# A fused attention-and-FFN kernel: more softmax tiles on VectorE, with the last integer shift of most batches done by an accumulating DMA

## The chip, the cores and the metric

One core of one Trainium2 chip. The metric is the device time of one execution in microseconds. A kernel was run four or more times beside runs of the kernel before on the same chip; medians are quoted. A ratio compares the mean times of two kernels' runs, matched by rounds, so it is not quite the ratio of the two medians that stand beside it. The profile shows one execution. Its span is some 2 us shorter than the time of the same run. In its views PE is TensorE, PEld are TensorE's weight loads, DVE is VectorE, ACT ScalarE, POOL GpSimd and SP SyncE; a number such as L904 is a line of the kernel. The granted clock is the share of TensorE's full clock that it was given.

## The reference

```python
x = A_x                                  # 1 x 2048 x 512, bf16
xn = _layernorm(x, axis=-1)
return x + _A_ref(xn, A_wq, A_wk, A_wv, A_wo) + _B_ref(xn, B_w1, B_b1, B_w2, B_b2)
# _A_ref: 32 query heads of 16, one shared key and value head;
#   p = softmax(q k^T * 16**-0.5);  o = p v;  o @ wo
# _B_ref: gelu(xn @ w1 + b1) @ w2 + b2, 1792 hidden columns
```

## The kernel before

The scores are made transposed, in tiles of 128 keys by 512 queries: 2048 tiles, in 683 units of three. A unit's three tiles lie in three banks of PSUM, the memory that PE writes to. ScalarE exponentiates them in one instruction, unless one of them is a "D tile". Then ScalarE takes only two, and VectorE makes the third: it rounds the scaled score to an integer whose bits are a coarse exponential in bf16, makes copies of it shifted by four constants, and PE multiplies each copy by a V that is scaled for it. The five products together approximate the exponential. `DTAB` says which units have a D tile (439 of them).

```python
SPL_K = (-51, -26, 0, 26, 51)            # the integer shifts; 0 is the PSUM pass itself

def p1(t, bk):                           # PSUM pass of one D tile
    ...
    dve(lambda e: e.tensor_scalar(Dt[:, KZ, s, :], bank(bk), float(127 * 128) + SPL_D, SPL_MIN, ALU.add, ALU.max), ...)

def close_batch():                       # up to three D tiles make a batch
    n = len(batch)
    s0 = batch[0][1]
    order = [KZ] + [k for k in range(len(SPL_K)) if k != KZ]
    for k in order:
        if k != KZ:
            dve(lambda e, k=k: e.tensor_scalar(Dt[:, k, s0:s0 + n, :], Dt[:, KZ, s0:s0 + n, :], float(SPL_K[k]),
                                               None, ALU.add), ...)
        for t, s in batch:               # PE: one product per copy and tile
            gg, kt, j = tile_of(t)
            pv_mm(gg, j, 1 + k, kt, Dt[:, k, s, :].bitcast(bf), [("D", s, k)])
```

Instructions are not issued in the order in which they are written: a list scheduler simulates all engines with estimates (`occ`, how long an instruction holds its engine, and `lat`, how long after that its result may be used) and writes out a fixed order for each engine. On the chip, an engine runs its instructions in that order, and semaphores make it wait where an estimate was too short. All of a group's products go into one PSUM accumulator.

Of the kernel before, what the change touches and what calls it, by code (L numbers as in the profile page):

```python
# [10 lines left out]
P = 128  # L11
# [27 lines left out]
NE_ND_KB = (25, 8, 3)  # L39
LA = 34  # L40
LB = 105
LY = 9
LP = 121
LS = 107
# [6 lines left out]
DTAB = "...00.20.0022.00.2...202202.22..0.200220..220..0.02.222002.20...2200220.2.0.2220.0...200000..002002.2.00..200220..00.200.0000....02.220.22.0220.02...2.22200022.0.2..220..20200220.20.20.220....22.200.2222.020020...2220.222.0222.0.020......2.2..0..020202....0220.20..0022.02.0...22..2220.2020.22.20...0.020020002...0020...02.00..0002202.022....222.2222.2222.0000..222.0.0222.022.200....00000.2020.00.02.2...22202.2.22.0000.000...2.2200.22..22.20.0...2.2.2.002..020020....220.2200.002.22.000....000020.2200.22200...02202.2.2002..2022...222220..0.2222.0020..22.00002.02.222020....20222...0202..0..2...220....2000.2.0.22....2.2.2.00..2.002020...0.00.2202.02000.00...20022.02.00.202000...."  # L51
# [7 lines left out]
YS = 9  # L59
HA = 40  # L60
HB = 165
# [365 lines left out]
def bass_parallel_sum__grouped_kv_mqa__dense_activation_gelu__prompt_kernel(  # L427
# [27 lines left out]
    NPR = 5  # L455
    NV = 1 + len(SPL_K)
    KZ = SPL_K.index(0)
    GAM = 128.0 / LN2 * 0.25
# [3 lines left out]
    with ExitStack() as es:  # L462
# [4 lines left out]
        ub = sb([P, FT, TBW], bf, "ub")  # L467
        xn = ub[:, 0:8, :]
        xnT = sb([P, DT, S], bf, "xnT")
        wvk = sb([P, DT, 2 * Dh], bf, "wvk")  # L470
        wkp = sb([P, DT, 4, 32], bf, "wkp")
        wq_sb = sb([P, DT, D], bf, "wq_sb")
        wqp = sb([P, DT, HG, 32], bf, "wqp")
# [31 lines left out]
        scr = sb([P, D], bf, "scr")  # L505
# [4 lines left out]
        ksq = sb([P, NT, Dh], f32, "ksq")  # L510
# [5 lines left out]
        Vf = sb([P, NT, Dh], f32, "Vf")  # L516
# [6 lines left out]
        Dt = sb([P, len(SPL_K), ND, TBW], i16, "Dt")  # L523
# [7 lines left out]
        oTp = sb([P, NPR, TBW], bf, "oTp")  # L531
# [41 lines left out]
        def dma(eng, o, i, stream, r=(), w=(), lat=2.2, allow=1.0, **kw):  # L573
            return add(eng, lambda e: e.dma_start(o, i), r, w, dma=stream, occ=0.7, lat=lat, allow=allow, **kw)
# [29 lines left out]
        dve(lambda e: e.memset(wkp[:], 0.0), w=["wkp"], n=256, due=0.0)  # L604
        dve(lambda e: e.memset(wqp[:], 0.0), w=["wqp"], n=512, due=0.1)
# [14 lines left out]
        for v, c in enumerate((1.0,) + SPL_C):  # L620
            setup(lambda e, v=v, c=c: e.memset(V1[:, v, :, Dh:Dh + 1], c), r=["V1"], w=["V1"], due=11.0)
        setup(lambda e: e.memset(sel8[:], 0.0), w=["sel8"], occ=0.3, due=12.0)
# [16 lines left out]
        def ln_batch(ts, how):  # L639
# [4 lines left out]
            if how == "a":  # L644
                for ti in ts:
                    act(lambda e, ti=ti: e.activation(scr[:], x_sb[:, ti, :], ACT.Identity, accum_out=sm[:, ti:ti + 1]),
                        r=[("x", ti)], w=["scr", ("sm", ti)], n=TBW + 250, due=land(ti))
                setup(lambda e: e.tensor_scalar(mean[:, sl], sm[:, sl], 1.0 / D, None, ALU.mult),
                      r=[("sm", ti) for ti in ts], w=mk, occ=0.2)
                setup(lambda e: e.tensor_scalar(nm[:, sl], sm[:, sl], -1.0 / D, None, ALU.mult),  # L650
                      r=[("sm", ti) for ti in ts], w=[("nm", ti) for ti in ts], occ=0.2)
                for ti in ts:
                    act(lambda e, ti=ti: e.activation(scr[:], x_sb[:, ti, :], ACT.Square, bias=nm[:, ti:ti + 1],
                                                      accum_out=sm[:, ti:ti + 1]),
                        r=[("x", ti), ("nm", ti)], w=["scr", ("sm", ti)], n=TBW + 250, due=land(ti))
                setup(lambda e: e.tensor_scalar(ve_b[:, sl], sm[:, sl], 1.0 / D, 1e-5, ALU.mult, ALU.add),
                      r=[("sm", ti) for ti in ts], w=[("ve", b)], occ=0.2)
            else:
                for ti in ts:
                    dve(lambda e, ti=ti: e.bn_stats(stats[:, ti, :], x_sb[:, ti, :]), r=[("x", ti)], w=[("st", ti)],  # L660
                        n=530, due=land(ti) + 1.0)
# [32 lines left out]
        def normed(ti):  # L694
            b, mean_ap = batch_of[ti]
            if XN_ENG[ti] == "d":
                dve(lambda e: e.tensor_scalar(xn[:, ti % 8, :], x_sb[:, ti, :], mean_ap, rstd[:, ti:ti + 1], ALU.subtract, ALU.mult),  # L697
                    r=[("x", ti), ("rstd", b), ("mv", b, ti)], w=[("u", ti % 8)], n=270, due=land(ti) + 2.0)
            else:
                act(lambda e: e.activation(xn[:, ti % 8, :], x_sb[:, ti, :], ACT.Identity, bias=nmr[:, ti:ti + 1],  # L700
                                           scale=rstd[:, ti:ti + 1]),
                    r=[("x", ti), ("rstd", b), ("nmr", b)], w=[("u", ti % 8)], n=TBW + 60, due=land(ti) + 2.0)

        def x_T(ts, bk, eng):
# [5 lines left out]
            for k, ti in enumerate(ts):  # L710
                for d in range(DT):
                    o = (d * n + k) * P
                    add("pe", lambda e, ti=ti, d=d, o=o: e.transpose(pT[:, o:o + P], xn[:, ti % 8, d * P:(d + 1) * P], ident[:]),  # L713
                        r=[("u", ti % 8), "ident"], w=[B(bk)], occ=0.085, due=land(ti) + 3.0)
# [95 lines left out]
        for v, c in enumerate(SPL_C):  # L810
            setup(lambda e, v=v, c=c: e.tensor_scalar(V1[:, 1 + v, :, 0:Dh], Vf[:], c, None, ALU.mult),
# [69 lines left out]
        def p1(t, bk):  # L881
            if not batch and dptr[0] + KB > ND:
# [4 lines left out]
            dve(lambda e: e.tensor_scalar(Dt[:, KZ, s, :], bank(bk), float(127 * 128) + SPL_D, SPL_MIN, ALU.add, ALU.max),  # L887
                w=[B(bk), ("D", s, KZ)], allow=P1_ALLOW, kind="p1")
# [7 lines left out]
        def close_batch():  # L896
            n = len(batch)
            s0 = batch[0][1]
            order = [KZ] + [k for k in range(len(SPL_K)) if k != KZ]
            for k in order:  # L900
                if k != KZ:
                    dve(lambda e, k=k: e.tensor_scalar(Dt[:, k, s0:s0 + n, :], Dt[:, KZ, s0:s0 + n, :], float(SPL_K[k]),  # L902
                                                       None, ALU.add),
                        r=[("D", s0 + i, KZ) for i in range(n)], w=[("D", s0 + i, k) for i in range(n)],  # L904
                        n=n * TBW, mode=4, allow=1.0, kind="post")
                for t, s in batch:
                    gg, kt, j = tile_of(t)
                    pv_mm(gg, j, 1 + k, kt, Dt[:, k, s, :].bitcast(bf), [("D", s, k)])
            del batch[:]

        onorm = {}

        def o_evac(gg):
# [20 lines left out]
            if h or end:  # L934
# [3 lines left out]
                                                r=keys, w=[("oTp", sl)], allow=3.0)  # L938
# [54 lines left out]

        def h_mm(tb, ft, ev=EV_ALLOW):
# [6 lines left out]
        def h_chain(tb, fts, al=3.0):  # L1001
# [3 lines left out]
            uu = ub[:, f0:f0 + n, :]  # L1005
            hk = [("h", s0 + i) for i in range(n)]
            uk = [("u", f) for f in fts]
# [8 lines left out]
        def y_mm(tb, i, start=True, stop=False, bk=7, fts=range(FT), al=1.5):  # L1016
            for ft in fts:
                mm4(bank(bk), ub[:, ft, i * P:(i + 1) * P], w2_sb[:, ft, :], start and ft == fts[0], stop and ft == fts[-1],
                   r=[("u", ft), "w2"], w=[B(bk)], allow=al)

        def wo_mm(tb, i, ps, start=False, bk=7, al=1.5):
            for n, p in enumerate(ps):
                pp = tb * NGR // 2 + p
                hs = [h for h in range(2) if 2 * pp + h < NTB * NGR - 1]
                assert all(2 * pp + h in onorm for h in hs)
# [6 lines left out]
        def store(tb, i):  # L1032
            ti = tb * 4 + i
            dma("sp", of[ti * P:(ti + 1) * P, :], x_sb[:, ti, :], f"d_o{i}", r=[("x", ti)], w=[("ob", i)])

        def out_tile(tb, i):
# [3 lines left out]
            ti = tb * 4 + i  # L1040
            dve(lambda e: e.tensor_tensor(x_sb[:, ti, :], pM, x_sb[:, ti, :], ALU.add), w=[("x", ti)] + M4, allow=EV_ALLOW)
            store(tb, i)

        xpy = x_sb[:, 0:8, :].rearrange("p t d -> p (t d)").bitcast(f32).rearrange("p (t d) -> p t d", d=D)

        def y_tile(tb, i):
            ti = tb * 4 + i
            y_mm(tb, i, al=YT_ALLOW[i])
            wo_mm(tb, i, range(FIN_G), al=YT_ALLOW[i])
            b2_mm(stop=i < 3, al=YT_ALLOW[i])  # L1050
            if i < 3:
                dve(lambda e: e.tensor_tensor(xpy[:, i, :], pM, x_sb[:, ti, :], ALU.add), r=[("x", ti)],
                    w=M4 + [("x", 2 * i), ("x", 2 * i + 1)], allow=EV_ALLOW)
            else:
                mm4(pM, ident, x_sb[:, ti, :], False, False, r=["ident", ("x", ti)], w=[B(7)], allow=YT_ALLOW[i])
# [22 lines left out]
        for tb in range(NTB):  # L1078
            u0 = tb * UPT
            if tb > 0:  # L1080
                for i in range(4):
                    at(u0 + 3 + (YS if tb < NTB - 1 else 9) * i, lambda tb=tb, i=i: out_tile(tb - 1, i), 0.6)
                q_at(tb, 3, u0 + Q3, (2, 3), (4, 5, 6, 7))
            a, b = (HA, HB) if tb < NTB - 1 else (LA, LB)
            if tb == 0:
                a = 18
            nf = FT if tb < NTB - 1 else FT - FIN_F
            for f0 in range(0, nf, 3):
                fts = list(range(f0, min(nf, f0 + 3)))
                for ft in fts:  # L1090
                    at(u0 + a + (b - a) * ft / FT, lambda tb=tb, ft=ft: h_mm(tb, ft), 0.6)
                at(u0 + a + (b - a) * fts[-1] / FT, lambda tb=tb, fts=fts: h_chain(tb, fts), len(fts) * 1.067 + 0.33)
# [3 lines left out]
            else:  # L1096
                for i in range(4):
                    at(u0 + LS + LY * i, lambda tb=tb, i=i: y_tile(tb, i), 0.6)
                fts = list(range(nf, FT))
                for ft in fts:  # L1100
                    at(u0 + LP + ft - nf, lambda tb=tb, ft=ft: h_mm(tb, ft), 0.6)
                if fts:
                    at(u0 + LP + len(fts), lambda tb=tb, fts=fts: h_chain(tb, fts, LAL), (len(fts) * 1.067 + 0.33) * LCO)
# [66 lines left out]
        for i in (0, 1, 3, 2):  # L1170
            ti = tb * 4 + i
            w = [(B(FB[i]), j) for j in range(4)] + ([B(FB[i])] if i < 3 else []) + [("x", ti)]
            if i < 3:
                dve(lambda e, i=i, ti=ti: e.tensor_tensor(x_sb[:, ti, :], bank(FB[i]), xpy[:, i, :], ALU.add),
                    r=[("x", 2 * i), ("x", 2 * i + 1)], w=w)
            else:
                act(lambda e, i=i, ti=ti: e.activation(x_sb[:, ti, :], bank(FB[i]), ACT.Copy), w=w)
            store(tb, i)
# [44 lines left out]
```

## Time and profile before

| | before |
|---|---|
| time, median of 4 runs | 797.58 us (796.94 to 798.07) |
| D tiles; batches | 439; 152 |
| exps of 1536 / of 1024 elements | 243 / 440 |
| shift instructions on VectorE | 608 |
| ScalarE idle in the span | 795.8 - 774.0 = 21.8 us |
| mean granted clock | 0.989 |

ScalarE sets the pace: it is full from 40 to 780 us, its 21.8 idle us lie in the prologue and the tail. The lines that carry this are in the prediction.

### The profile page before, as it was taken

The page shows a single profiled execution, that of the slowest core. Times are in us where ns is not written, and L with a number is a line of the kernel's source. Part 1 is how long each engine was busy: PE and PEld are TensorE (multiplying, and loading weights), DVE is VectorE, ACT ScalarE, POOL GpSimd, SP SyncE. Part 2 cuts the span into 40 slices and gives each one's busy share as a digit, 9 for nine tenths or more (in the row PEclk, how much of TensorE's full clock was granted, in tenths as well). Part 3 has the DMA queues.
Part 4 walks back from the last instruction along what each step waited for, and adds up shares of the span by engine and source line. Part 5 has one row for each costly group of instructions (what it writes and reads, how often), then busy time and mean ns, then how long its engine had stood idle before and what let it go on. Part 6 is the DMA issues. An engine that isn't in the chain of part 4 may idle for free.

```text
span 795.8 us, 20778 instructions
## 1 busy us (share of the span) xinstructions
PE 767.0 (96%) x8759; PEld 240.5 (30%) x8759; DVE 739.8 (93%) x1401; ACT 774.0 (97%) x734; POOL 20.8 (3%) x84
## 2 busy tenths in 40 slices
PE   6799999999999999999999999999999999999998
PEld 4323322232222323322232233322233233323222
DVE  8589999999998959999999889999999998999896
ACT  4899999999999999999999999999999999999995
POOL 6300000000000000000000000000000000000000
PEclk7899999999999999999999999999999999999999
DMA  9101100000000010001000001100001010000001
GB/s 312 41 9 30 23 15 16 17 21 13 12 22 23 23 29 16 17 15 22 17 13 24 20 19 23 22 16 16 19 12 22 24 22 23 16 9 16 16 9 35
DMA packets 30007, 21.17 MB, mean 27 GB/s; under 512 B 16353, under 2 KB 25434, under 8 KB 29914
## 3 DMA queue, kind: packets, MB, share of 16 engines
q1 hardware_dynamic: 28330, 19.28, 9.4%
q8 instruction: 69, 1.13, 0.6%
q10 hardware_dynamic: 1584, 0.56, 0.3%
q14 instruction: 24, 0.20, 0.1%
HBM read 10.98 MB, written 2.35 MB: 17 GB/s over the span
## 4 chain that ended last, share of the span: by engine, by line
ACT 92%; PE 5%; DVE 3%; DMA 0%; issue 0%; DVEq 0%
ACT E L870 88%; ACT ub L1012 3%; PE pAll L891 2%; PE pAll L851 1%; DVE stats L660 1%; PE pAll L567 1%; PE pAll L561 1%; DVE Dt L887 0%; DVE Dt L902 0%; DMA x_sb<-in_A_x_dram 0%; ACT xnT L718 0%; PE pAll L713 0%; ACT KT L732 0%; ACT ub L700 0%; DVE ub L697 0%
## 5 line engine op out<-in xcount | busy, mean ns | idle before, releaser
L870 ACT ACTIVATE E<-pAll 128x1024 bf16<-128x1024 f32 (+1 forms) x683 | 736.7, 1335 | 1.5 <-PE pAll L851 1.3
L891 PE MATMUL pAll<-Dt,V 128*32 128x512 bf16 x2195 | 390.0, 383 | 0.3
L887 DVE TENSOR_SCALAR Dt<-pAll 128x512 int16<-128x512 f32 x439 | 292.9, 680 | 28.9 <-PE pAll L851 28.3
L891 PE MATMUL pAll<-E,V 128*32 128x512 bf16 x1609 | 303.2, 387 | 1.4 <-DVE Of L915 1.2
L902 DVE TENSOR_SCALAR Dt<-Dt 128x1536 int16<-128x1536 int16 (+1 forms) x608 | 297.6, 533 | 0.9
L851 PE MATMUL pAll<-QT,KT 32*128 32x512 bf16 x2048 | 268.3, 386 | 15.0 <-ACT E L870 8.4
L851 PEld LDWEIGHTS pAll<-QT,KT 32*128 32x128 bf16 x2048 | 68.8, 91 | 290.4 <-ACT E L870 222.9
L891 PEld LDWEIGHTS pAll<-Dt,V 128*32 128x32 bf16 x2195 | 105.6, 94 | 107.0 <-issue 54.8
L567 PE MATMUL pAll<-xnT,w_sb 128*32 128x512 bf16 x896 | 128.1, 382 | 0.1
L567 PE MATMUL pAll<-w_sb,ub 128*32 128x512 bf16 x896 | 125.4, 382 | 0.0
L891 PEld LDWEIGHTS pAll<-E,V 128*32 128x32 bf16 x1609 | 70.7, 93 | 77.0 <-issue 59.1
L567 PE MATMUL pAll<-wop,oTp 128*32 128x512 bf16 x256 | 50.8, 381 | 0.0
L998 DVE TENSOR_SCALAR hb<-pAll,b1T 128x512 bf16<-128x512 f32 x56 | 41.5, 740 | 0.8 <-PE pAll L891 0.5
L567 PEld LDWEIGHTS pAll<-xnT,w_sb 128*32 128x32 bf16 x896 | 33.6, 95 | 24.1 <-issue 10.0
L567 PEld LDWEIGHTS pAll<-w_sb,ub 128*32 128x32 bf16 x896 | 32.1, 95 | 11.8 <-issue 5.2
L1184 PE MATMUL pAll<-xnT,zeros 128*32 128x512 bf16 x308 | 33.1, 383 | 0.0
L1012 ACT ACTIVATE ub<-ub 128x1536 bf16<-128x1536 bf16 (+1 forms) x20 | 32.1, 1606 | 0.0
L915 DVE COPY Of<-pAll 128x512 f32<-128x512 f32 x31 | 21.1, 680 | 5.0 <-PE pAll L567 4.1
L567 PE MATMUL pAll<-xnT,wq_sb 128*32 128x512 bf16 x256 | 20.5, 398 | 0.0
L1011 DVE TENSOR_TENSOR ub<-ub,hb 128x1536 bf16<-128x1536 bf16 (+1 forms) x20 | 17.9, 893 | 0.1
L1014 DVE TENSOR_TENSOR ub<-ub,hb 128x1536 bf16<-128x1536 bf16 (+1 forms) x20 | 17.9, 894 | 0.1
L1009 DVE TENSOR_TENSOR ub<-hb 128x1536 bf16<-128x1536 bf16 (+1 forms) x20 | 17.8, 892 | 0.1
(124 smaller groups left out, 242.7 us busy)
## 6 DMA issues: line engine op xcount, KB each, us to landing
OfP<-Of SPq DMA_DIRECT2D x124, 32.0 KB, 1.9
rbP<-rden_rows SPq DMA_DIRECT2D x124, 32.0 KB, 1.8
w_sb<-in_B_w_dram SPq DMA_DIRECT2D x2, 1792.0 KB, 13.5
x_sb<-in_A_x_dram SPq DMA_DIRECT2D x8, 256.0 KB, 6.1
out_dram<-x_sb SPq DMA_DIRECT2D x16, 128.0 KB, 1.7
QT<-qp SPq DMA_DIRECT2D x124, 16.0 KB, 1.8
wq_sb<-in_A_wq_dram ACTq DMA_DIRECT2D x1, 512.0 KB, 6.5
wop<-in_A_wo_dram SPq DMA_DIRECT2D x1, 512.0 KB, 16.3
```

The costliest lines, as they stand in the source:

```text
L567: add("pe", lambda e, c=c, j=j: e.matmul(o[c, :], l[:, c], rh, start=start, stop=stop, tile_position=(0, 32 * j)), r, [(k, j) for k in w] ...
L851: ins = e.matmul(o, l, rh, start=True, stop=True, tile_position=(q0, 0))
L870: exps.append(act(lambda e: e.activation(E[:, s0:s0 + na, :], bank(b0, na).rearrange("p (a n) -> p a n", a=na), ACT.Exp, scale=LN2 / 128.0 ...
L887: dve(lambda e: e.tensor_scalar(Dt[:, KZ, s, :], bank(bk), float(127 * 128) + SPL_D, SPL_MIN, ALU.add, ALU.max), w=[B(bk), ("D", s, KZ)], ...
L891: add("pe", lambda e, a, b: e.matmul(pO[32 * j:32 * j + 32, :], V1[:, v, kt, :], rhs, start=a, stop=b, tile_position=(0, 32 * j)), r=r + [ ...
L902: dve(lambda e, k=k: e.tensor_scalar(Dt[:, k, s0:s0 + n, :], Dt[:, KZ, s0:s0 + n, :], float(SPL_K[k]), None, ALU.add), r=[("D", s0 + i, KZ ...
L915: dve(lambda e: e.tensor_copy(Of[:, i, :], pO), w=["O", ("Of", i)], allow=0.0)
L998: dve(lambda e: e.tensor_scalar(hb[:, ft % 6, :], pM, b1T[:, ft:ft + 1], None, ALU.add), r=["b1T"], w=M4 + [("h", ft % 6)], allow=ev)
L1011: dve(lambda e: e.tensor_tensor(uu, uu, hh, ALU.mult), r=uk + hk, w=uk, n=c, mode=2, allow=al)
L1012: act(lambda e: e.activation(uu, uu, ACT.Tanh, scale=GELU_K), r=uk, w=uk, n=c, allow=al - 0.5, kind="tanh")
L1014: dve(lambda e: e.tensor_tensor(uu, uu, hh, ALU.mult), r=uk + hk, w=uk, n=c, mode=2, allow=al)
L1184: pr.filler = lambda e, j, o: e.matmul((pO if o else pM)[32 * j:32 * j + 32, :], zeros[:, 0:32], xnT[:, 0, 0:TBW], start=not o, stop=not o ...
```

## The change

The intent is to move more exponentials from ScalarE to VectorE, and to pay for it by taking work off VectorE: in most batches the fourth shift is done by a DMA that adds a constant row to the first copy, in place, once the first copy's products have been read. The rest makes room for that: four copies in place of five, twelve slots in place of eight, two FFN activation buffers (the second over x, whose rows are loaded again when they are needed), so that the FFN's work can be spread.

```diff
-DTAB = "...00.20.0022.00.2...          (cut; 439 D tiles)
+DTAB = "....2.002002222.00...          (cut; 473 D tiles)
-NE_ND_KB = (25, 8, 3)
+NE_ND_KB = (22,12,3)
+HP = ((18,160),(180,320),(330,470),(480,590))      # where the FFN's parts go
+YP = (...)
+DM_T = 40                        # the DMA serves batches that end at tile 40 or earlier of a group's 64
+DM_LAT = 4.0
+DM_OCC = 1.0
 ...
-        def dma(eng, o, i, stream, r=(), w=(), lat=2.2, allow=1.0, **kw):
+        def dma(eng, o, i, stream, r=(), w=(), lat=2.2, allow=1.0, accum=False, **kw):
+            if accum:
+                return add(eng, lambda e: e.dma_start(o, i, accum_op=ALU.add), r, w, dma=stream, occ=DM_OCC, lat=lat, allow=allow, **kw)
 ...
+            setup(lambda e: e.memset(kst[:], SPL_K[KORD[-1]]), w=["kst"], occ=0.4, due=12.0)
 ...
+            by_dma = batch[-1][0] % TPG <= DM_T
+            for step, k in enumerate(KORD):
+                b = min(step, len(KORD) - 2)
+                if 0 < step < len(KORD) - 1:
+                    dve(... Dt[:, b, s0:s0 + n, :] = Dt[:, 0, ...] + SPL_K[k] ...)          # shortened
+                elif step:
+                    b = 0
+                    if by_dma:
+                        dma("pool", Dt[:, 0, s0:s0 + n, :], kst[:].unsqueeze(1).to_broadcast([P, n, TBW]), f"d_sh{s0}", r=["kst"], w=[(q, 0) for q in keys],
+                            lat=DM_LAT, accum=True)
+                    else:
+                        dve(lambda e, k=k: e.tensor_scalar(Dt[:, 0, s0:s0 + n, :], Dt[:, 0, s0:s0 + n, :], float(SPL_K[k]), None, ALU.add), ...)
                 for t, s in batch:
                     gg, kt, j = tile_of(t)
-                    pv_mm(gg, j, 1 + k, kt, Dt[:, k, s, :].bitcast(bf), [("D", s, k)])
+                    pv_mm(gg, j, 1 + k, kt, Dt[:, b, s, :].bitcast(bf), [(("D", s), b)])
 ...                              # (cut: second buffer, reload of x, aliased scratch)
```

`DM_OCC` and `DM_LAT` are what the scheduler takes the DMA to need: 1.0 + 4.0 = 5.0 us from its start on GpSimd until PE may read the result. 107 of 169 batches use it, all of three tiles (384 KB).

## The prediction

> **What bounds the kernel now.** I read the page's busy shares first, then the windows (busy time of each engine in stretches of the run), then the chain that ended last, the costliest groups, the waits, and a stretch of VectorE's timeline. The busy shares alone name three suspects:
>
> ```profile
> PE 767.0 (96%) x8759; PEld 240.5 (30%) x8759; DVE 739.8 (93%) x1401; ACT 774.0 (97%) x734; POOL 20.8 (3%) x84
> ```
>
> The windows (columns: stretch, length, then busy us and instruction count of PE, PEld, DVE, ACT, POOL, then clock, DMA share, GB/s) separate them:
>
> ```profile
> 40.00:100.00 60.00, 58.66 (x635) 18.05 (x634) 57.44 (x113) 59.95 (x57) 0.00 (x0) 1.00 0.09 21
> ...
> 200.00:300.00 100.00, 98.64 (x1204) 29.46 (x1203) 87.95 (x169) 100.00 (x94) 0.00 (x0) 1.00 0.09 21
> 300.00:400.00 100.00, 98.49 (x1055) 30.13 (x1054) 98.86 (x185) 100.00 (x94) 0.00 (x0) 1.00 0.08 17
> 400.00:500.00 100.00, 99.47 (x1211) 30.29 (x1211) 92.21 (x179) 100.00 (x95) 0.00 (x0) 1.00 0.08 20
> 500.00:600.00 100.00, 97.39 (x1056) 29.48 (x1054) 99.01 (x180) 99.40 (x93) 0.00 (x0) 1.00 0.07 17
> ...
> 764.00:780.00 16.00, 15.39 (x188) 4.36 (x188) 15.30 (x29) 16.00 (x17) 0.00 (x0) 1.00 0.06 14
> ```
>
> ScalarE is full from 40 to 780 us. VectorE swings between 88% and 99%: idle while the FFN's second matmul runs, full while the FFN's activation chain runs. GpSimd does nothing. The chain of waits agrees, and the groups say what the ScalarE work is:
>
> ```profile
> ACT E L870 88%; ACT ub L1012 3%; PE pAll L891 2%; PE pAll L851 1%; DVE stats L660 1%; PE pAll L567 1%; PE pAll L561 1%; DVE Dt L887 0%; DVE Dt L902 0%; DMA x_sb<-in_A_x_dram 0%; ACT xnT L718 0%; PE pAll L713 0%; ACT KT L732 0%; ACT ub L700 0%; DVE ub L697 0%
> ```
> ```profile
> L870 ACT ACTIVATE E<-pAll 128x1024 bf16<-128x1024 f32 x440 | 447.3, 1189 | 0.8 <-PE pAll L851 0.6
> ...
> L870 ACT ACTIVATE E<-pAll 128x1536 bf16<-128x1536 f32 x243 | 364.3, 1599 | 0.7 <-PE pAll L851 0.7
> L887 DVE TENSOR_SCALAR Dt<-pAll 128x512 int16<-128x512 f32 x439 | 292.9, 680 | 28.9 <-PE pAll L851 28.3
> L902 DVE TENSOR_SCALAR Dt<-Dt 128x1536 int16<-128x1536 int16 x548 | 277.4, 548 | 0.9
> ```
>
> The softmax runs in 683 units of three 128x512 score tiles. In a unit without a D tile ScalarE exponentiates all three (1536 wide); in one with a D tile it does two (1024), and VectorE makes the third by integer arithmetic: one pass from PSUM, then shifted copies. So the time is set by how many units carry a D tile, and VectorE's time sets how many can. PE is busy but waits: its weight loads for the scores stood 222.9 us behind ScalarE in sum, so PE has slack.
>
> ```profile
> PEld pAll L851 <- ACT E L870: 222.9, 525, 1.9
> ```
>
> VectorE's real cost per instruction is the distance between starts, not the duration, since neighbours overlap. In the timeline two wide shifts take 777.18 - 776.24 = 0.94, so 0.47 us each, and a PSUM pass 776.24 - 775.64 = 0.60 us:
>
> ```profile
> 775.64 0.68 DVE L887 TENSOR_SCALAR Dt<-pAll 128x512 int16<-128x512 f32 x1
> 776.24 1.02 DVE L902 TENSOR_SCALAR Dt<-Dt 128x1536 int16<-128x1536 int16 x2
> 777.18 1.28 DVE L887 TENSOR_SCALAR Dt<-pAll 128x512 int16<-128x512 f32 x2
> ```
>
> **What the Trainium skill says.** "ScalarE: Activation LUTs", What ACT_TABLE_LOAD costs: about 186 ns plus 0.833 ns per element, so 512 elements fewer save 427 ns. The trace's means differ by 1599 - 1189 = 410 ns; I use 0.41. "DMA: Bandwidth & Descriptors", SWDGE vs HWDGE vs iDMA: a DMA that accumulates can be issued only by GpSimd, whose cores write the descriptors in software; the same page (Anatomy of one DMA) gives 2.0 us plus bytes over 436 GB/s. For 128x1536 int16 (384 KB) that is 2.9 us as a plain copy. The trace of before has no such DMA to compare. "SBUF - State Buffer", The "DVE blocks DMA" trap: while VectorE runs a two-port fast mode, GpSimd can't write descriptors, and the lock works both ways. The shifts (int16, SBUF to SBUF, 0.47 us for 1536 elements, which is more than three elements a cycle at 0.96 GHz) are in such a mode; the passes from PSUM are not. No conflict shows in before, because GpSimd idles throughout the loop.
>
> **The change, part by part.** Counts are from the table of D tiles and the instruction order of the two programs.
>
> 1. ScalarE: D tiles go from 439 to 473. 34 units fall from 1536 to 1024 elements: 34 x 0.41 = 13.9 us less on the engine that sets the pace. The tanh work is unchanged (20 instructions). This is the only direct saving.
> 2. VectorE: 34 more PSUM passes, 34 x 0.60 = +20.4 us. Shift instructions go from 608 to 569: wide ones 548 to 477, -71 x 0.47 = -33.4; 1024-wide 52 to 48, about -1.3; single-tile ones 8 to 44, about 0.20 each (duration 0.28 less the same 0.08 overlap), +7.2. Sum -7.1 us. That is what the DMA buys: 107 of 169 batches have their fourth shift done by it, and without it 107 x 0.47 = 50 us would come on top, which wouldn't fit.
> 3. VectorE's share: 688.8 us busy between 40 and 764 in before (57.4+99.2+88.0+98.9+92.2+99.0+93.4+39.7+21.0), 95% of 724. Afterwards about 682 in 710, 96%. It fits only if it is even. That is what the second activation buffer does: the next block's chain no longer waits for the output tiles to read the first buffer, so chain and output tiles can be spread. D tiles in sixteenths of the run lie between 23 and 30 in before and between 27 and 32 after.
> 4. PE: 170 more matmuls with D tiles, 34 fewer with E, +136. Four run side by side, so about 0.22/4 = 0.054 us each (0.22 us per matmul is in the chain): +7.3 us. The fillers, which only keep the clock up, fall from 308 to 116: -10.4 us. About even; PE keeps its slack.
> 5. DMA: 107 x 384 KB, two reads and one write; plus 16 reloads of x rows (128 KB) issued six units ahead of use. The loop's DMA share is below 0.10, so there is room. What counts is latency. In PE's order the matmuls that read the DMA's result stand behind 8 to 13 score visits (median 11) counted from the batch's last D unit. A visit runs about three units ahead of ScalarE, so that is some 8 units, 8.3 us, at 1.04 us a unit. Three shifts, and other VectorE work between them, take 2 to 4 us of it. About 4 to 5 us are left for issue to landing.
> 6. Rings: D slots go from 8 (two batches of three fit) to 12 (four), with four copies in place of five; E slots from 25 to 22. A batch is needed about every 3/0.69 = 4.3 units, so four batches give some 18 us from reuse to reuse: enough for a DMA of 5 us.
>
> Prologue and tail are nearly unchanged: the aliased scratch buffers are dead when the new owner writes, and the last batches of a group keep their shift on VectorE. So 797.7 - 13.9 = 783.8 us is the clean outcome.
>
> I add 1 us. The steps of the 1024-wide exps are not all at their floor: they are 0.904 us at the median and 0.92 in the mean without the few stalls, some 9 us over the loop, caused by late scores. 34 more such units, on fuller engines, won't have fewer. Prediction: 785 us.
>
> **Rivals.**
> A: the DMA is late. PE runs in order, so a matmul that waits for the landing holds the scores behind it, and ScalarE runs dry. For it: software descriptors, 384 row pieces (the constant row is read three times per partition), a read-modify-write, and the lock. An estimate from 2.9 us, about 0.9 more for the second read and 1 us of descriptor writing is 4.8 us, at the edge of the 4 to 5 us. One microsecond too late in each of 107 batches, half of it absorbed, gives +50 us: about 835. Against it: the schedule has reserved 5 us, and such a loss would hardly have been kept in a tuned kernel.
> B: the lock makes VectorE the bound. If each descriptor write holds up VectorE by 0.2 us, 107 x 0.2 = 21 us of its 28 us of idle time goes, and waits leak to ScalarE: 788 to 795. For it: shifts are a third of VectorE's time. Against: the DMA is issued just after the batch's own shifts, when PSUM passes are likely to come.
> C: spreading also removes ScalarE's waits. At most the 9 us above: down to 777. Against: the waits are short and scattered, not in the stages where VectorE is full.
>
> **Range and chances.** 785 is 1.6% faster. The 2% line is at 781.8, which needs 16 us, 2 more than the clean saving, so a part of C must come true: 0.24. Slower by over 2% (over 813.7) needs A in earnest: 0.07. The rest, 0.69, is within 2%. Range for 8 in 10: 778 to 796, longer upward because of B.
>
> **What would show it.** Right: exp groups x474 and x209 with unchanged means and ScalarE at 100% in every window of the loop; VectorE even at 95 to 97%; the accumulating DMA landing in under 5 us; almost no PE wait on it. Wrong: PE weight loads waiting for the D tile's DMA (A); shift durations above 548 ns, or a mean well above it beside GpSimd work (B); 1024-wide exps well below or above 1189 ns (C, or new stalls); E's share of the chain falling below 85%.

## More of the kernel before

One line is added here for later, from the page's list of DMA issues (size of one, then median us from issue to landing). It is a small transfer of the softmax's normalisation, issued by SyncE:

```profile
rbP<-rden_rows SPq DMA_DIRECT2D x124, 32.0 KB, 1.8
```

## The result, and the profile after

The kernel became slower: 816.23 us (814.35 to 817.99, four runs) against 797.58, ratio 1.0234 with a 95% interval of 1.0203 to 1.0265. This lies outside the predicted range of 778 to 796.

The busy line of the page after, and the chain that ended last, by engine and by line:

```profile
PE 769.0 (95%) x8703; PEld 237.9 (29%) x8703; DVE 740.4 (91%) x1396; ACT 766.3 (94%) x734; POOL 175.8 (22%) x192
```
```profile
PE 45%; DMA 19%; DVE 17%; ACT 16%; issue 1%; POOL 1%; SPq 0%; DVEq 0%; ACTq 0%; POOLq 0%
PE pAll L904 21%; DMA Dt<-kst 17%; ACT E L883 14%; PE pAll L864 13%; PE pAll L576 9%; DVE Dt L900 7%; DVE Dt L917 4%; DVE hb L1024 1%; DMA wq_sb<-in_A_wq_dram 1%; POOL Dt L584 1%; DMA rden_rows<-den 1%; DMA rbP<-rden_rows 1%; PE pAll L570 1%; DVE Of L938 1%; ACT ub L713 1%
```

ScalarE's exps, 88% of the chain before, are 14% now. The path runs through PE and the new DMA. ScalarE's idle time has grown from 21.8 to 813.0 - 766.3 = 46.7 us. The windows (same columns as in the prediction) say that it is spread over the loop, and that VectorE is not full where ScalarE loses most:

```profile
100.00:200.00 100.00, 97.63 (x1023) 29.21 (x1024) 96.77 (x180) 98.74 (x94) 17.55 (x13) 1.00 0.42 68
200.00:300.00 100.00, 95.40 (x1100) 28.30 (x1098) 94.63 (x178) 96.33 (x94) 21.14 (x14) 1.00 0.47 77
...
400.00:500.00 100.00, 94.67 (x1080) 28.54 (x1072) 89.30 (x167) 93.99 (x90) 23.00 (x16) 0.98 0.52 84
...
600.00:700.00 100.00, 97.28 (x1174) 29.00 (x1174) 88.51 (x162) 94.71 (x89) 18.90 (x14) 0.98 0.44 75
```

From 400 to 500 us ScalarE (the fourth busy figure) has 93.99 of 100 and VectorE 89.30, where before they had 100.00 and 92.21. So no engine is full, which is the mark of waiting and not of work.

The groups, by form (busy us, mean ns, then idle before it and what ended most of that):

```profile
L883 ACT ACTIVATE E<-pAll 128x1024 bf16<-128x1024 f32 x474 | 461.1, 1082 | 20.4 <-PE pAll L864 19.4
...
L883 ACT ACTIVATE E<-pAll 128x1536 bf16<-128x1536 f32 x209 | 300.0, 1504 | 7.4 <-PE pAll L864 7.4
...
L917 DVE TENSOR_SCALAR Dt<-Dt 128x1536 int16<-128x1536 int16 x438 | 229.3, 558 | 0.7
```

The counts 474 and 209 are those predicted. ScalarE now stands idle for 27.8 us before its exps, 26.8 of them for scores (L864); before, it was 1.5 us. The means fall although nothing is faster: from start to start, the 1024-wide ones take 0.904 us at the median in both traces. Their durations include the time that they share with the exp before, and that is less now: 58 exps start with no overlap (4 before), and the other 1024-wide ones overlap by 0.17 us in the mean (0.27 before). The waits name what held the scores up (us in total, times, longest):

```profile
PEld pAll L904 <- DMA Dt<-kst: 40.9, 51, 2.9
...
ACT E L883 <- PE pAll L864: 26.8, 36, 2.5
...
PE pAll L904 <- DMA Dt<-kst: 21.8, 24, 2.4
```

PE's weight loads stood for the DMA's result 51 times, 40.9 us in all. The third line is not more of it. It shows the same waits at the matmuls, which the weight loads run ahead of: all 24 lie within the 51, and the matmuls were idle for 21.8 us of the 40.9. (The expectations below add the two lines and speak of 63 us; that counts a wait twice. From here on the waits are those of the weight loads.) PE runs in order, so the score matmuls behind such a wait are late too. The DMA issues and the view of the constant row say how long the DMA takes:

```profile
Dt<-kst POOLq DMA_DIRECT2D x107, 384.0 KB, 5.1
...
rbP<-rden_rows SPq DMA_DIRECT2D x124, 32.0 KB, 2.7
```
```profile
L584 POOL DMA_DIRECT2D Dt<-kst x107: 1273/1332/3755, 46.5 to 795.4; - x107
...
DMA to landing us min/median/max: 4.6/5.1/7.3
```

The first numbers of the second fence are the time on GpSimd in ns, minimum, median and maximum: writing the descriptors. From start to landing it is 5.1 us at the median (5.3 in the mean over the 107), with a tail to 7.3. The reserve is 5.0.

One such wait in full. VectorE's timeline, GpSimd's, then PE's weight loads, its matmuls, and ScalarE's (start, us, instruction, in brackets the idle time before and what ended it):

```profile
702.63 3.43 DVE L917 TENSOR_SCALAR Dt<-Dt 128x1536 int16<-128x1536 int16 x8
705.98 0.55 DVE L926 TENSOR_SCALAR Dt<-Dt 128x1536 int16<-128x1536 int16 x1
```
```profile
704.29 3.75 POOL L584 DMA_DIRECT2D Dt<-kst  x1 [3.49 <-DVE Dt L917]
```
```profile
711.45 0.10 PEld L904 LDWEIGHTS pAll<-Dt,V 128*32 128x32 bf16 x3 [2.87 <-DMA Dt<-kst]
```
```profile
707.93 0.39 PE L864 MATMUL pAll<-QT,KT 32*128 32x512 bf16 x3
...
711.45 0.61 PE L904 MATMUL pAll<-Dt,V 128*32 128x512 bf16 x3 [2.38 <-DMA Dt<-kst]
712.00 0.61 PE L864 MATMUL pAll<-QT,KT 32*128 32x512 bf16 x3
```
```profile
712.65 1.02 ACT L883 ACTIVATE E<-pAll 128x1024 bf16<-128x1024 f32 x1 [2.38 <-PE pAll L864]
715.09 1.02 ACT L883 ACTIVATE E<-pAll 128x1024 bf16<-128x1024 f32 x1 [1.41 <-PE pAll L864]
```

The DMA starts at 704.29, while VectorE runs shift after shift. Its descriptors take 3.75 us in place of 1.3, and it lands at 711.45, after 7.2 us. The scores of the next unit go out at 712.00, four microseconds after those before them (707.93). ScalarE is idle for 2.38 us and then for 1.41 more. In the second gap PE is busy but slower: a matmul that took 0.39 us takes 0.61 after the wait. The windows of this stretch show it in the clock (the figure after the five engines):

```profile
700.00:706.00 6.00, 6.00 (x91) 1.89 (x89) 6.00 (x14) 6.00 (x6) 2.51 (x2) 1.00 0.46 68
706.00:712.00 6.00, 3.62 (x47) 1.02 (x40) 2.20 (x5) 4.27 (x4) 2.05 (x1) 0.92 0.44 66
712.00:716.00 4.00, 4.00 (x31) 1.10 (x32) 2.46 (x4) 1.94 (x2) 0.52 (x1) 0.69 0.05 8
```

The Trainium skill, "TensorE: Matmul & The Clock Gate", What's actually happening, says that PE's clock is halved after at least one window of about 3.4 us in which PE was idle. The trace agrees on the halving: the 0.69 is a mean, and a view of 711.10 to 714.40 alone gives 0.50. It doesn't agree on the length: the weight loads had waited for 2.87 us and the matmuls for 2.38. In the loop this happened three times, after the three longest of the 51 waits.

### The profile page after: what moved, and what is told of

Its sections match the earlier page's. It is cut to its first block, busy times and chain, and to the rows that moved or that the text cites. A ratio compares the mean times of both kernels' runs of the same rounds, so it can differ in the third digit from the quotient of the medians.

```text
span 813.0 us, 20872 instructions
## 1 busy us (share of the span) xinstructions
PE 769.0 (95%) x8703; PEld 237.9 (29%) x8703; DVE 740.4 (91%) x1396; ACT 766.3 (94%) x734; POOL 175.8 (22%) x192
## 4 chain that ended last, share of the span: by engine, by line
PE 45%; DMA 19%; DVE 17%; ACT 16%; issue 1%; POOL 1%; SPq 0%; DVEq 0%; ACTq 0%; POOLq 0%
PE pAll L904 21%; DMA Dt<-kst 17%; ACT E L883 14%; PE pAll L864 13%; PE pAll L576 9%; DVE Dt L900 7%; DVE Dt L917 4%; DVE hb L1024 1%; DMA wq_sb<-in_A_wq_dram 1%; POOL Dt L584 1%; DMA rden_rows<-den 1%; DMA rbP<-rden_rows 1%; PE pAll L570 1%; DVE Of L938 1%; ACT ub L713 1%
## 5 line engine op out<-in xcount | busy, mean ns | idle before, releaser
L883 ACT ACTIVATE E<-pAll 128x1024 bf16<-128x1024 f32 (+1 forms) x683 | 725.7, 1211 | 27.8 <-PE pAll L864 26.8
L904 PE MATMUL pAll<-Dt,V 128*32 128x512 bf16 x2365 | 409.4, 387 | 22.4 <-DMA Dt<-kst 21.8
L900 DVE TENSOR_SCALAR Dt<-pAll 128x512 int16<-128x512 f32 x473 | 314.9, 680 | 39.4 <-PE pAll L864 35.4
L584 POOL DMA_DIRECT2D Dt<-kst x107 | 154.5, 1453 | 603.8 <-PE pAll L904 259.3
L864 PE MATMUL pAll<-QT,KT 32*128 32x512 bf16 x2048 | 269.9, 388 | 6.8 <-ACT E L883 3.4
L917 DVE TENSOR_SCALAR Dt<-Dt 128x1536 int16<-128x1536 int16 (+2 forms) x507 | 249.1, 530 | 0.7
L864 PEld LDWEIGHTS pAll<-QT,KT 32*128 32x128 bf16 x2048 | 68.0, 91 | 270.6 <-ACT E L883 162.1
L576 PE MATMUL pAll<-w_sb,ub 128*32 128x512 bf16 x448 | 63.4, 382 | 0.0
L576 PE MATMUL pAll<-w_sb,x_sb 128*32 128x512 bf16 x448 | 59.9, 382 | 0.0
L926 DVE TENSOR_SCALAR Dt<-Dt 128x1536 int16<-128x1536 int16 (+2 forms) x62 | 28.1, 476 | 0.2
L576 PE MATMUL pAll<-b2row,ones 128*32 128x512 bf16 x64 | 21.0, 392 | 0.0
L576 PEld LDWEIGHTS pAll<-w_sb,ub 128*32 128x32 bf16 x448 | 17.5, 95 | 5.9 <-issue 1.4
L576 PEld LDWEIGHTS pAll<-w_sb,x_sb 128*32 128x32 bf16 x448 | 15.9, 95 | 9.4 <-issue 5.4
```

Source lines behind the costliest of these rows:

```text
L576: add("pe", lambda e, c=c, j=j: e.matmul(o[c, :], l[:, c], rh, start=start, stop=stop, tile_position=(0, 32 * j)), r, [(k, j) for k in w] ...
L584: return add(eng, lambda e: e.dma_start(o, i, accum_op=ALU.add), r, w, dma=stream, occ=DM_OCC, lat=lat, allow=allow, **kw)
L864: ins = e.matmul(o, l, rh, start=True, stop=True, tile_position=(q0, 0))
L883: exps.append(act(lambda e: e.activation(E[:, s0:s0 + na, :], bank(b0, na).rearrange("p (a n) -> p a n", a=na), ACT.Exp, scale=LN2 / 128.0 ...
L900: dve(lambda e: e.tensor_scalar(Dt[:, 0, s, :], bank(bk), float(127 * 128) + SPL_D, SPL_MIN, ALU.add, ALU.max), w=[B(bk), (("D", s), 0)], ...
L904: add("pe", lambda e, a, b: e.matmul(pO[32 * j:32 * j + 32, :], V1[:, v, kt, :], rhs, start=a, stop=b, tile_position=(0, 32 * j)), r=r + [ ...
```

## The experiments

The theory after the first look: the DMA lands, in about half of the batches, a little later than PE's fixed order reads it, and nothing else of the change costs much (T1). Rivals: the DMA's traffic and the lock between VectorE's shifts and descriptor writing slow the engines as such (T2); or the new table of D tiles, with the spread side work, is itself worse (T3).

**e1_reserve: a longer reserve, the table left alone.**

```diff
-DM_LAT = 4.0
+DM_LAT = 6.5
```

> The changed kernel with the scheduler told that the accumulating DMA takes 2.5 us longer (7.5 us from issue in place of 5.0), so that PE's fixed order reads its result later; nothing else changes in number or kind. Theory A (the DMA lands later than PE's order assumed, PE stalls in order, ScalarE runs dry): PE's wait on the DMA falls from 63 us to under 15, ScalarE's exp steps come back to the floor, time 784 to 792. Theory B (descriptor writing and VectorE's fast modes lock each other out, or the traffic slows the other DMAs): no gain from the order, time stays above 808.

Measured: 837.13 us (835.37 to 839.32), ratio 1.0496 (1.0473 to 1.0519). A miss. The waits show that the edit did what it was to do, and that it made another wait:

```profile
ACT E L883 <- PE pAll L864: 39.9, 44, 3.0
...
PEld pAll L904 <- DMA Dt<-kst: 4.7, 4, 2.3
...
PE pAll L904 <- DMA Dt<-kst: 3.3, 2, 2.0
```

PE's waits on the DMA fell from 40.9 to 4.7 us, but ScalarE waited 39.9 us for scores that the new order itself places late. A table of D tiles is made for one set of estimates. With another estimate the scheduler finds an order of its own, with other collisions, and here a much worse one. One sign of it is in the profile: the scheduler fills PE time that it expects to be idle with matmuls on zeros, 536 of them here and 116 in the changed kernel. That the late products crowd the end of each group, where the accumulator must be complete, is my guess; no run shows it. So this run doesn't test T1, and from here on I keep the order fixed where I can.

**e2_nowait: the same order, the DMA runs as before, but nothing waits for it.** Its output is wrong, which doesn't matter for the time. The last products read another finished copy, which is the wrong shift. (The check of the result against the reference didn't catch this or e5; both are wrong by construction.)

```diff
-                    pv_mm(gg, j, 1 + k, kt, Dt[:, b, s, :].bitcast(bf), [(("D", s), b)])
+                    if by_dma and step == len(KORD) - 1:
+                        pv_mm(gg, j, 1 + k, kt, Dt[:, 3, s, :].bitcast(bf), [(("D", s), 0), (("D", s), 3)])
+                        op = pr.ops[-1]
+                        op.deps = [o for o in op.deps if o.eng != "pool"]
+                    else: ...             # as before
```

> Wrong result on purpose: the same instructions in the same order, the DMA runs as before, but the last matmuls of such a batch read the copy that VectorE had shifted third and don't wait for the DMA. Theory A: the wait alone is the cost, time 783 to 790. Theory B: all traffic and locking is still there, so time stays near 816.

Measured: 785.17 us (784.67 to 786.75), ratio 0.9847 (0.9832 to 0.9862). The DMA is still there, and as slow as before (5.1 us to landing); ScalarE's wait is gone:

```profile
L883 ACT ACTIVATE E<-pAll 128x1024 bf16<-128x1024 f32 x474 | 467.7, 1148 | 4.1 <-PE pAll L864 3.7
...
L584 POOL DMA_DIRECT2D Dt<-kst x107 | 156.8, 1478 | 578.2 <-PE pAll L904 246.3 <-DVE Dt L917 134.0 <-PE pAll L864 87.4
```

So 816.2 - 785.2 = 31 us come from the wait alone. T2 falls: all traffic, descriptor writing and locking are in this kernel. T3 falls as the cause of the slowness: table, buffers and spread are in it too.

**e5_third: the same order and the same waits, a shorter DMA.** Its output is wrong, which doesn't matter for the time. The DMA adds to one of the three tiles.

```diff
-                        dma("pool", Dt[:, 0, s0:s0 + n, :], kst[:].unsqueeze(1).to_broadcast([P, n, TBW]), ...
+                        dma("pool", Dt[:, 0, s0:s0 + 1, :], kst[:].unsqueeze(1).to_broadcast([P, 1, TBW]), ...
```

> Wrong result on purpose: same order and same waits, but each accumulating DMA works on one of the three tiles (128 KB, 128 pieces). Theory A (PE waits because the DMA lands later than reserved): landing falls under 4 us, PE's wait on it under 5 us, time 783 to 790. Theory B': what costs is that the matmuls hang on a POOL instruction at all (its start waits on PE and VectorE), not how long the DMA takes: then most of the loss stays, over 803.

Measured: 783.49 us (783.18 to 784.21), ratio 0.9823 (0.9807 to 0.9839). From the DMA issues and the waits:

```profile
Dt<-kst POOLq DMA_DIRECT2D x107, 128.0 KB, 2.9
```
```profile
PEld pAll L904 <- DMA Dt<-kst: 2.3, 3, 1.0
```

Here every wait is still in the program; the DMA is only in time. The trace also gives the number that the prediction lacked. As nothing waits, the distance from a DMA's start on GpSimd to PE's first read of its result is the place that PE's order gives it: 4.9 us at the median of the 107, from 4.2 to 6.8, with a tenth below 4.4. In the changed kernel the landing takes 4.6 to 7.3. The two ranges lie on top of each other.

The page's ScalarE figures of the two kernels also say where 813.0 - 782.0 = 31.0 us of span went. Idle time: 46.7 against 782.0 - 759.7 = 22.3, so 24.4 us. The other 6.6 us are busy time (766.3 against 759.7) for the same instructions. That fits the exps which start after idle time: 58 in the changed kernel and 5 here. Without an overlap an exp of 1024 elements takes 1.02 us, 0.12 more than from start to start, and 53 x 0.12 = 6.4 us.

**e4_wide and e4_rows2: the right result, with fewer descriptors.** The constant row of 512 elements is read three times per partition, in 384 pieces. A row of 1536, read once, didn't fit into SBUF, so e4_wide was never run.

> The constant is 128x1536, so source rows are 3 KB and not three times 1 KB (one E slot less for the room). If landing time is set by the number of row pieces (384 a DMA), descriptor writing falls well below 1.3 us and landing from 5.1 to about 4 us; then theory A expects most of PE's 63 us of waiting to go and 790 to 800 us. If bytes or the fixed part set it, landing stays near 5 us and the time near 816.

In its place, a row of 768 elements read twice (256 pieces), with the order unchanged:

```diff
-        kst = sb([P, TBW], i16, "kst") if DM_T >= 0 else None
+        kst = sb([P, 3 * TBW // 2], i16, "kst") if DM_T >= 0 else None
 ...
-   Dt[:, 0, s0:s0 + n, :], kst[:].unsqueeze(1).to_broadcast([P, n, TBW])
+   Dt[:, 0, s0:s0 + 3, :] viewed as [P, 2, 768], kst[:].unsqueeze(1).to_broadcast([P, 2, 3 * TBW // 2])
```

> The changed kernel, instruction order unchanged, with a constant row of 768 elements read twice per partition in place of 512 read three times: 256 row pieces a DMA and not 384, same bytes. If the number of pieces sets descriptor writing, its floor falls from 1.27 to about 0.85 us and the median landing from 5.1 to about 4.6 us; theory A then expects some 40% of the 31 us of lost ScalarE time back, 800 to 806 us. If it does not change the landing, about 816.

Measured: 806.44 us (803.52 to 811.41), ratio 1.0121 (1.0076 to 1.0167). The descriptor writing fell only from 1.27 to 1.20 us at its fastest, less than I had thought; the landing fell by about 0.3 us, to 4.8, and PE's waits on it from 40.9 to 32.5 us. The time just missed the expected 800 to 806. So 0.3 us of landing moved the kernel by 10 us: the ends of the DMA and the reads are that close. Together with e5 it is a dose and its response, at a fixed order: landing 5.1, 4.8, 2.9 us; time 816.2, 806.4, 783.5.

**e3_nodma: the changed kernel with all four shifts on VectorE.** `DM_T = -1`, table unchanged.

> The changed kernel with the fourth shift of all batches on VectorE (no DMA), same table of 473 D tiles. VectorE gets 107 x 0.47 = 50 us more than in the changed kernel: 740 us of busy time become 790. Theory A and B alike: VectorE becomes the bound, about 805 to 825; if it comes out under 797, the DMA was never needed for this table.

Measured: 815.72 us (813.46 to 816.99), ratio 1.0227 (1.0202 to 1.0251).

```profile
PE 772.4 (95%) x8855; PEld 248.0 (31%) x8855; DVE 777.9 (96%) x1503; ACT 763.0 (94%) x734; POOL 20.9 (3%) x84
```

VectorE's busy time is 777.9 us, 37.5 more than with the DMA where 50 were expected, and with this table it is too full for 473 D tiles. So the DMA does take work off VectorE, but as delivered, its lateness costs just what it saves: 816.2 with it, 815.7 without. As in e1 the order is another one, with a table that was made with the DMA in the plan. What a table searched without it would give was not tested.

**e8_oldtable: the rest of the change by itself.** No DMA, and the table of the kernel before (439 D tiles).

> The changed kernel without any DMA shift and with the D table of before (439 tiles): what is left is the two activation buffers, the spread side work, the in-place ring of 12 slots and the reloading of x. The clean reckoning (ScalarE sets the pace, same exp work as before) says 795 to 800; if the structure alone loses time, over 803. The table was made for the other arrangement of side work, so up to 10 us more from that would not surprise.

Measured: 801.45 us (800.92 to 802.90), ratio 1.0050 (1.0035 to 1.0065). This lies between the two expected ranges. Two buffers, spread side work, the in-place ring and the reload of x give nothing by themselves; with a table that wasn't made for them they cost 4 us.

**e6_early and e7_early2: issue the DMA earlier.** The result stays right: the last copy is made from copy 1 (already shifted by -51) by adding 102. e7 has the row of 768 too. The order on PE is unchanged.

```diff
-  kst = SPL_K[KORD[-1]]                 Dt[:, 0, ...] += kst
+  kst = SPL_K[KORD[-1]] - SPL_K[KORD[1]]    Dt[:, 1, ...] += kst     (shortened)
```

> Right result, instruction order on every engine unchanged, same DMA size: the DMA adds 102 to the copy that VectorE shifted first (-51, so it ends at +51) and not 51 to the unshifted copy. It then needs to wait only for the first of the three shifts and for PE's reading of that copy, so it can start earlier while PE's place for the result stays. Theory A (landing later than PE's place in the order): with 1 to 2 us more lead most of the 63 us of PE waits go, 785 to 795. If the DMA's start is held by PE's reading of the first copy rather than by the shifts, the lead is small and the time stays over 805.

> The same with the constant row of 768 elements read twice (256 row pieces), which made landing 0.28 us shorter. Theory A: a little better than e6_early, 784 to 792.

Measured: e6 821.33 us (820.67 to 823.34), ratio 1.0301 (1.0283 to 1.0318); e7 810.54 us (808.46 to 814.20), ratio 1.0169 (1.0135 to 1.0204). Both missed: they are slower than the same kernels without the edit (816.2 and 806.4). GpSimd's line points to the reason:

```profile
L584 POOL DMA_DIRECT2D Dt<-kst x107 | 156.4, 1465 | 610.0 <-PE pAll L864 246.6 <-PE pAll L904 162.1 <-DVE Dt L900 106.9
```

A DMA that overwrites a copy can't start before PE has read that copy, and most of GpSimd's idle time was ended by PE (246.6 + 162.1 of 610.0 us). The early start was hardly to be had: measured against PE's weight loads, whose order is the same, the DMAs of e6 start 0.2 us earlier at the median than in the changed kernel, not 1 to 2 us. PE's waits on the DMA were 42.0 us, against 40.9 without the edit. So these two runs don't test T1 either; what they show is that an in-place DMA is bound to its readers at both ends. Why e6 is 5 us slower than the changed kernel is open.

**e9 to e12: plan for what the DMA really takes.** If T1 is right, a larger reserve must pay as soon as the D table is made for it, which e1 didn't do. I searched the table anew, with the kernel's own scheduler as the judge, for three reserves. The edits against the changed kernel:

| | reserve (`DM_OCC` + `DM_LAT`) | row | D tiles, of them batches by DMA |
|---|---|---|---|
| e9_replan | 1.4 + 4.6 = 6.0 us | 512 x 3 | 475, 105 |
| e10_replan_rows2 | 6.0 us, the same table | 768 x 2 | 475, 105 |
| e11_replan575_rows2 | 1.25 + 4.5 = 5.75 us | 768 x 2 | 473, 105 |
| e12_replan66_rows2 | 1.4 + 5.2 = 6.6 us, `DM_T = 36` | 768 x 2 | 469, 93 |

> The changed kernel with the same DMA (384 KB, three row pieces per partition, in place on the unshifted copy), but the D table was searched anew with 6.0 us reserved from issue to landing in place of 5.0: 475 D tiles in place of 473, 105 DMAs in place of 107. e1_reserve changed the reserve alone, with a table made for the old one, and lost by it. Theory A: landing stays at 5.1 us median, PE's wait on it falls from 63 us to under 20 (only the tail of landings over 6 us still waits), time 784 to 794, faster than before. Rival: the in-order PE cannot take a DMA into its path whatever is planned, time stays over 800.

> e9_replan with the constant row of 768 elements read twice, which cut landing by 0.28 us without costing anything else. Theory A: a little under e9_replan, 782 to 791.

> As e10, with a table searched for 5.75 us reserved (473 D tiles, 105 DMAs). Less margin than e10 by 0.25 us: theory A expects PE's wait on the DMA somewhat above e10's and the time within 3 us of it, 783 to 793.

> As e10, with a table searched for 6.6 us reserved and the DMA only for batches ending at tile 36 of 64 or before: 469 D tiles, 93 DMAs, four or six D tiles fewer than e11 and e10 (some 2 us of ScalarE). Theory A: the reserve now covers about 95 in 100 landings of e10 (its 90th percentile is 5.9 us), PE's wait on the DMA under 8 us, and as few stalls also keep the clock up, 785 to 792, steadier from run to run than e10. If the time stays at 794 or above with the waits gone, something else than the landing holds the re-planned kernels back.

| | time, us | ratio to before (95%) | PE's waits on the DMA, us |
|---|---|---|---|
| changed kernel, 5.0 | 816.23 (814.35 to 817.99) | 1.0234 (1.0203 to 1.0265) | 40.9 |
| e9, 6.0 | 799.64 (798.66 to 800.98) | 1.0024 (1.0007 to 1.0041) | 18.0 |
| e11, 5.75, rows of 768 | 795.45 (792.70 to 802.13) | 0.9992 (0.9938 to 1.0046) | 12.5 |
| e10, 6.0, rows of 768 | 794.05 (791.05 to 798.39) | 0.9957 (0.9920 to 0.9994) | 7.7 |
| e12, 6.6, rows of 768 | 792.93 (791.58 to 797.23) | 0.9940 (0.9927 to 0.9952) | 1.8 |

All four times lie above their expected ranges (e12's by 0.9 us); the waits came out as expected. The DMA itself is unchanged (5.1 us to landing in e9, 4.8 in the others). What changed is where PE reads it. The waits and the time fall together, and e12, the best, beats both kernels: 792.93 against 816.23 and against 797.38 of its own rounds, which is still within 2% of the kernel before. As each reserve has its own table, not every microsecond of this can be put down to the reserve alone, and a new search at the old 5.0 us, which might have found a better table too, was not run; but e9 and e10 share a table, and there 0.3 us of landing are again worth 5.6 us.

e12 is still 7.5 us above what the prediction's reckoning gives for 469 D tiles (797.7 - 30 x 0.41 = 785.4), with hardly a wait on this DMA. Its profile, which fell on the slowest of its six runs (797.23), shows a part of what is left:

```profile
ACT E L883 <- PE pAll L864: 11.9, 15, 1.5
...
DVE oTp L960 <- DMA rbP<-rden_rows: 4.6, 2, 2.9
```
```profile
101.88 0.69 DVE L960 TENSOR_TENSOR oTp<-OfP,rbP 128x512 bf16<-128x512 f32 x1 [1.61 <-DMA rbP<-rden_rows]
...
103.15 1.28 DVE L900 TENSOR_SCALAR Dt<-pAll 128x512 int16<-128x512 f32 x2
```
```profile
103.89 0.10 PEld L864 LDWEIGHTS pAll<-QT,KT 32*128 32x128 bf16 x3 [2.14 <-DVE Dt L900]
```

The second fence is VectorE's timeline, the third that of PE's weight loads. VectorE runs in order too. At 101.88 it had stood for the small normalisation DMA, so its next PSUM pass came late, and PE, which needs that bank for new scores, stood 2.14 us. This looks like the same fault on another estimate, but it is one wait. The small DMA's landing rose from 1.8 us before to 2.7 in the changed kernel and in e9, and was 1.9 in e5, with a third of the traffic; in e12 it is 1.9 at the median too, and the four before this wait took 1.8 to 3.0 us. The clock is another part: it stood at half in three stretches of e12's loop, 13.6 us in all, in which ScalarE was idle for 4.0.

## Why the prediction was wrong

- **What bounds the kernel, and step 1 (13.9 us saved on ScalarE).** Right. The exps are 474 and 209 as counted, and without the wait the kernel takes 785.17 us (e2) against the 785 predicted. With the shorter DMA it takes 783.49 (e5), against the clean 783.8. The 0.41 us a unit is a difference of durations; from start to start it is 1.330 - 0.904 = 0.43 at the median, which makes 14.5 us.
- **Step 2 and step 3 (VectorE holds, if evenly loaded).** Right in kind. The shift counts are as reckoned, e2 has 473 D tiles and all passes of the changed kernel, and ScalarE waits 4.8 us in its exps. VectorE's busy time fell by less than the 7.1 us of the sum: from 739.8 to 737.7 in e2 and 734.2 in e5. In e3, without the DMA, 473 D tiles don't fit with this table, as the step said.
- **Step 4 (PE keeps its slack).** Right as far as work goes: e2's PE has the same instructions and holds ScalarE up by 4.4 us. But the 222.9 us that the prediction read as slack are waits of the weight loads, which run ahead; in before, the score matmuls themselves stood for ScalarE for 8.4 us only.
- **Step 5 (the DMA's latency). This is the step that failed.** Both of its sizes were near: "About 4 to 5 us are left for issue to landing", and 4.9 us are; 4.8 us for the landing in rival A, and 5.1 it is. What failed is the conclusion. I set a typical landing against a typical room and let them pass as fitting. With equal centres, about half of all batches are late, and each late one stops the engine that feeds ScalarE: 51 waits, 40.9 us. A landing with a tail to 7.3 us needs a reserve for its tail; 5.0 us is below even its median.
- **Rival A.** It had the mechanism word for word. Its size was an assumption: one microsecond in each of 107 batches, half of it absorbed, about 50 us. Measured were 40.9 us of waiting, in 51 waits, of which 31 us (816.2 - 785.2) became time. So there was less waiting than assumed, and a quarter of it was absorbed and not half. I gave it 0.07, for one reason: "the schedule has reserved 5 us, and such a loss would hardly have been kept in a tuned kernel". That is no evidence. A reserve in a scheduler is the author's belief about a duration, and the trace of before held no DMA of this kind to check it by.
- **Step 6 (the rings).** Four batches in the ring were enough: in e2, with the DMA at its full length, VectorE waited for it once, 0.5 us. The 18 us were not the binding interval; the one from start to read was.
- **Rival B (the lock makes VectorE the bound).** Wrong on the side that suffers. The wide shifts take 558 ns in the mean, 548 before, and e2 leaves for lock and traffic together about the 1.4 us between 785.2 and the clean 783.8, which is itself an estimate. It is the descriptor writing that is stretched, 1.27 to 3.75 us, when VectorE runs many shifts in a row. This makes part of the tail (7 of the 16 landings over 6 us had over 1.7 us of it), so it belongs to A. What made the other nine late is not shown.
- **Rival C (spreading removes waits).** Not seen: e8 shows no gain from the rest of the change.
- **Range.** It ended at 796 because only B widened it. A's 835 was in the text but not in the range.

Open: how much of e12's remaining 7.5 us is late small DMAs, and how much is the clock that falls after some of the waits; why e1's order is so much worse; how much a new table alone gives; and whether another table would reach the clean 785 with a right result.

## What to carry to other kernels

Where engines run in a fixed order, a new asynchronous step is not hidden because it is shorter than the room on average: compare the tail of its latency with the shortest room, since each miss stops everything behind it. Before you trust a scheduler's estimate for an operation that the profile doesn't show, treat it as unmeasured and let the range hold the case that it is too short. And to test such a theory, keep the order and shorten or remove the wait (e2, e5); changing the estimate alone (e1) changes the whole order, and tests something else.

## What the Trainium skill lacked or had wrong

- "DMA: Bandwidth & Descriptors", Anatomy of one DMA: its fit gives 2.9 us for 384 KB. The accumulating DMA from SBUF to SBUF landed after 5.1 us (107 in the changed kernel, 4.6 to 7.3), and one of 128 KB after 2.9, where the fit gives 2.3. Of the landing, 1.33 us at the median are descriptor writing for 384 KB and 0.87 for 128 KB, so the rest grows by about (5.1 - 1.33) - (2.9 - 0.87) = 1.7 us for 256 KB more: some 150 GB/s (an estimate) in place of 436, for a transfer that reads two rows for each that it writes. The page has no figure for an accumulating DMA.
- The table of the same section calls the time of descriptor generation small and variable and has no figure by the number of pieces. On GpSimd it was at least 0.87, 1.20 and 1.27 us for 128, 256 and 384 pieces (e5, e4, changed kernel).
- "SBUF — State Buffer", The "DVE blocks DMA" trap: the runs agree that VectorE's fast operations keep GpSimd from writing descriptors. What the page doesn't say is that a row of them holds one DMA up over several instructions, and which side pays in a full loop: writing the descriptors of one DMA took up to 3.75 us in the changed kernel and 5.16 us in e6, in place of 1.27, while no slowing of VectorE's shifts is visible (558 ns against 548).
- "TensorE: Matmul & The Clock Gate", HAM oscillation: its rule is that PE must not be idle for longer than about 3.4 us. In the changed kernel one wait of 2.87 us (2.38 at the matmuls) was followed by a clock of 0.50, with matmuls of 0.61 in place of 0.39 us; in e10 a wait of 1.74 us was, with clocks of 0.50 and 0.52 in the ten microseconds after it. Most waits were not: in the changed kernel 3 of 51 were, the shortest of them 2.19 us, and a wait of 2.15 us was not.
- No page tells how much small DMAs of SyncE suffer beside such transfers: the landing of a 32 KB one rose from 1.8 to 2.7 us at the median in the changed kernel (2.4 in e4 and 1.9 in e12).
